# Three weight parts narrowed early and read back, the spread of 1/root on ScalarE, and the rows stored from ScalarE's queue

## The chip, the cores and the metric

One core of a Trainium2 chip runs the kernel; the other cores are idle. The metric is the time of one execution on the device in microseconds (us). Engines: PE (TensorE, matmuls), DVE (VectorE), ACT (ScalarE), POOL (GpSimd), SP (SyncE, which here only starts DMAs). Each engine carries out its own instructions in a fixed order, and they wait for one another on semaphores.

## The reference

Three stages, each the input of the next, in float32. The output of the third, 1792 rows of 768, is the result.

```python
# attention with a sigmoid: 4 batches, 12 heads, 448 positions, 64 wide
scores = scale * np.matmul(q, k.transpose(0, 1, 3, 2)) - np.log(S)
attn = 1.0 / (1.0 + np.exp(-scores))
x = np.matmul(attn, v)                       # then laid out as 1792 x 768
# gated dense layer (768 -> 1536 -> 768)
xn = x / np.sqrt(np.mean(x * x, axis=-1, keepdims=True) + 1e-06) * rms_g
g = xn @ w_gate
x = (g * (1.0 / (1.0 + np.exp(-g))) * (xn @ w_val)) @ w_out
# routed experts: 8 experts (768 -> 1024 -> 768), each row goes to its best one
logits = x @ w_gate2
e = np.argmax(logits, axis=1)                # gate_w = softmax(logits)[e]
out[row] = gate_w[row] * (np.maximum(x[row] @ w1[e], 0.0) @ w2[e])
```

## The kernel before

The work goes batch by batch. `moe1(b)` is the dense layer of batch b: 12 units that each make one slice of the gate (`pg`, by `w_gate`) and of the value (`pv`, by `w_val`), and then 6 output units (`oc` 0 to 5, bank `py`, by `w_out`). A unit has 4 pieces of 9 matmuls, a batch 72 pieces. Every product of float32 numbers is made of three matmuls over high and low parts (`three`, L299 to L301). The attention of batch b + 1 is spread over the pieces of batch b (`attention_due`), its matmuls between those of the dense layer. PE therefore has one order, written out by the Python code: whoever is late makes PE wait. `later(k, f)` puts f behind the k-th next piece.

PE's results lie in banks of PSUM. The dense layer has three banks `mm`, and in the output units one of them holds the logits of the routing (`logit_bank`), so that `py` goes back and forth between two, and so do the first units of the next batch until the logits are copied (L398).

The weights of the dense layer come as 64-bit words, 36 parts of 768 KB (`load_64`; two parts for each unit, 33 to 35 are the last of `w_out`). DVE narrows each part to float32 by three operations (L221, L225, L229), which the generator `conversions` gives out one at a time. 24 of the 108 stand in the attention of batch 0, then `operations_due(n)` after each piece n of batch 0. Parts 0 to 11 and 14 to 19 are held in the tiles h0 to h11, which later take the hidden values `hs`; the others pass through a ring of four. Each narrowed part is stored to DRAM (`w32d`), and batches 1 to 3 load it from there (`load_32`, L244). A part is then split: ACT casts the high part `wh` (L252), DVE subtracts the low part `wl` (L255).

What ends a gate's piece: ACT takes the sigmoid of the bank (L307), DVE multiplies (L308), and with that the bank is free. For a value: L313 on DVE, L314 on ACT, L315 on DVE. For an output unit: ACT copies the bank (`x2s`, L340), DVE makes its low part (L343) and a transposed copy `xr` (L346); SP stores `x2s` (L353), and after every second unit `rows` starts four DMAs that store `xr`, which has one buffer, as rows (L380). `logits` (L385) multiplies `x2s` one unit later.

The end of an attention: PE sums the squares `ss` of `x` into `pm` (L786), DVE begins 1/root (`va`, L791 to L799), and for b > 0 POOL refines it (L806 to L809, `ya`); DVE spreads it to `yb` (L814); PE turns `yb` into `prs` (L818), and `x` is scaled by it (L827 on DVE, L830 on ACT, L821 on DVE). In the routed experts L904 is ACT's activation of the first matmuls.

Every DMA that SP or ACT starts takes the next of eight semaphores in turn. Where the earlier DMA on that semaphore can still be under way, the engine that issues waits for its landing first.

Of the kernel before, what the change touches and what calls it, by code (L numbers as in the profile page):

```python
# [19 lines left out]
B, H, S, D = 4, 12, 448, 64  # L20
# [4 lines left out]
KF = FF // 128  # L25
# [3 lines left out]
CT = 112  # L29
NC = S // CT  # L30
# [9 lines left out]
NU = KF + KD  # L40
SP = mybir.EngineType.SP

HELD = 12

RAW = 3

RQK = 2
# [13 lines left out]

def operations_due(n):

    return 2 if n % 4 == 3 else 1


CONST = {}
# [31 lines left out]
def f32(ap):  # L99
    return ap.bitcast(F32)  # L100
# [3 lines left out]
def block_kernel(ctx, tc, qkp, qk, v, wg, wv, wo, g, gate, w1, w2, consts, out):  # L104
    nc = tc.nc
# [61 lines left out]
    def later(ticks, f, *a):  # L167

        due.setdefault(clock[0] + ticks, []).append((f, a))

    def tick():
        clock[0] += 1
        for f, a in due.pop(clock[0], []):
            f(*a)
# [22 lines left out]
    w64, w32, spl = {}, {}, {}  # L197

    def part_of(c):

        u, i = divmod(c, 2)
        if u < KF:
            return (wg, wv)[i][u]
        return wo[u - KF, :, KD * i : KD * i + KD]

    def load_64(c):
        r = rp.tile([128, DM, 2], I32, tag="w64", name="w64", bufs=RAW)
        words = part_of(c).rearrange("p c k -> p (c k)").bitcast(I32)
        nc.sync.dma_start(out=r, in_=words.rearrange("p (n t) -> p n t", t=2))
        w64[c] = r  # L210

    def narrow(c):

        r = w64.pop(c)
        lo, hi = r[:, :, 0], r[:, :, 1]
        if place[c] is not None:
            w = wp.tile([128, DM], F32, tag=f"h{place[c]}", name="w32h")
        else:
            w = wp.tile([128, DM], F32, tag="w32", name="w32", bufs=4)
        u = w.bitcast(I32)  # L220
        nc.vector.tensor_scalar(  # L221
            out=u, in0=hi, scalar1=3, scalar2=0x3FFFFFF8, op0=ALU.logical_shift_left, op1=ALU.bitwise_and
        )
        yield
        nc.vector.scalar_tensor_tensor(  # L225
            out=u, in0=lo, scalar=29, in1=u, op0=ALU.logical_shift_right, op1=ALU.bitwise_or
        )
        yield
        nc.vector.scalar_tensor_tensor(  # L229
            out=u, in0=hi, scalar=-0x40000000, in1=u, op0=ALU.bitwise_and, op1=ALU.bitwise_or  # L230
        )
        w32[c] = w
        if c < HELD:
            to_store.append((c, w))
        else:
            later(1, lambda: nc.sync.dma_start(out=w32d[c // 2][c % 2], in_=w))
        x = order.index(c) + RAW
        if x < 2 * NU:
            later(2 if c < 8 else 3, load_64, order[x])
        yield  # L240

    def load_32(n, i):
        w = wp.tile([128, DM], F32, tag="w32", name="w32", bufs=4)
        nc.sync.dma_start(out=w, in_=w32d[n % NU][i])  # L244
        w32[2 * n + i] = w

    def split_w(n, i):
        w = w32.pop(2 * n + i)
        h = wp.tile([128, KD, 128], F32R, tag="wh", name="wh", bufs=3)
        l = wp.tile([128, KD, 128], F32R, tag="wl", name="wl", bufs=3)  # L250
        w3 = w.rearrange("p (c k) -> p c k", k=128)
        nc.scalar.copy(out=h, in_=w3)  # L252

        def low():
            nc.vector.tensor_tensor(out=l, in0=w3, in1=f32(h), op=ALU.subtract)  # L255
            split_done[0] += 1
            if NU <= n + 1 < NU * B:
                load_32(n + 1, i)

        later(1, low)  # L260
        spl[n, i] = (h, l)

    place = {c: c if c < HELD else c - 8 if 14 <= c < 20 else None for c in range(2 * NU)}
    round_of = [c for c in range(2 * NU) if place[c] is None]
    order = list(range(14)) + [20, 21] + list(range(14, 20)) + list(range(22, 2 * NU))
    split_done = [0]
    to_store = []

    def conversions():
        for c in order:
            if place[c] is not None:
                before = c - 8 if c >= HELD else -1
            else:
                x = round_of.index(c)
                before = round_of[x - 4] if x >= 4 else -1
            while split_done[0] <= before:
                yield False
            for _ in narrow(c):  # L280
                yield True

    conv = conversions()

    def ahead(n, piece):
# [19 lines left out]
    def moe1(b):  # L305
# [32 lines left out]
        def out_copy(p, oc):  # L338
            h, l = (keep.tile([128, S], F32R, tag=f"x2_{k + oc % 2}", name="x2s") for k in (2, 4))
            nc.scalar.copy(out=h, in_=p)  # L340

            def rest():
                nc.vector.tensor_tensor(out=l, in0=p, in1=f32(h), op=ALU.subtract)  # L343
                if oc % 2 == 0:
                    pair[0] = keep.tile([128, S // 32, 2, 32], F32, tag="xr", name="xr")
                nc.vector.transpose(out=pair[0][:, :, oc % 2, :], in_=p.rearrange("p (j a) -> p j a", a=32))  # L346

            later(1, rest)
            x2_t[b, oc] = None, h, l

            def store():
                for k, x in enumerate((h, l)):
                    nc.sync.dma_start(out=x2s[b][k * KD + oc], in_=f32(x))  # L353
                if oc % 2:
                    rows(b, oc - 1, pair[0])

            later(2, store)
# [17 lines left out]
    def rows(b, oc, xr):  # L375

        to = x2d[0][b * S : (b + 1) * S, :DM].rearrange("(j a) (i r) -> i a j r", a=32, i=4)
        to = to[:, :, :, 32 * oc : 32 * oc + 64]
        for i in range(4):
            nc.sync.dma_start(out=to[i], in_=xr[32 * i : 32 * i + 32].rearrange("a j o r -> a j (o r)"))  # L380

    def logits(b, oc):

# [164 lines left out]
    def attention(b):  # L548
# [202 lines left out]
        for t in range(n_steps + 4 if b > 1 else 0):  # L751
            if t < n_steps:
                h, c = divmod(t, NC)
# [31 lines left out]
        for c in range(NC):  # L785
# [3 lines left out]
        ya = aq.tile([CT, NC], F32, tag="ya", name="ya")  # L789
# [4 lines left out]
            out=ta.bitcast(I32), in0=va.bitcast(I32), scalar1=1, scalar2=None, op0=ALU.logical_shift_right  # L794
        )
        nc.vector.tensor_scalar(
            out=ya.bitcast(I32), in0=ta.bitcast(I32), scalar1=-1.0, scalar2=float(0x5F3759DF), op0=ALU.mult, op1=ALU.add
# [13 lines left out]
            yield  # L811
            yield
        yb = aq.tile([CT, NC, 128], F32, tag="yb", name="yb")
        nc.vector.tensor_copy(out=yb, in_=ya.unsqueeze(2).to_broadcast([CT, NC, 128]))  # L814
        yield
        pr = sc_bank([128, S], "prs")
        for c in range(NC):
# [5 lines left out]
        before = None  # L823
        for c in range(KD):
# [3 lines left out]
                out=xt[c], in0=xt[c], scalar=g_sb[:, c : c + 1], in1=pr, op0=ALU.mult, op1=ALU.mult  # L828
# [4 lines left out]
            before = c, xh, xl  # L833
# [361 lines left out]


    att = {b: attention(b) for b in range(B)}
    for n in range(QS + 2):
        next(att[0])
        if n < RAW:  # L1200
            load_64(n)
# [4 lines left out]
        if n == 15:  # L1206
            nc.scalar.copy(out=gate_2[:, :, :E], in_=gate_sb)
            nc.vector.tensor_tensor(
                out=gate_2[:, :, E:], in0=gate_sb, in1=f32(gate_2[:, :, :E]), op=ALU.subtract
# [7 lines left out]
    for _ in att[0]:  # L1217
        tick()
        next(att[1])
        ahead_of += 1  # L1220
    gated.append(True)
    for b in range(B):
# [3 lines left out]
        for n, _ in enumerate(moe1(b)):  # L1226
            want = attention_due(b, n)
            while done < want:
                next(steps, None)
                done += 1  # L1230
            tick()
            if b == 0:
                if to_store:
                    c, w = to_store.pop(0)
                    nc.sync.dma_start(out=w32d[c // 2][c % 2], in_=w)
                for _ in range(operations_due(n)):
                    next(conv, None)
            elif n >= 2 and n % 2 == 0:
                next(routing, None)
            if b == 3:  # L1240
                if n == 0:
                    s_a.close()
                    s_r.close()
                    open_raw()
                    load_x(0)
                    e0 = own_expert(0)
                if n >= 2 and n % 2 == 0 and n < 2 * KD + 2:
                    load_row(w1, ph2["w1r"], e0, n // 2 - 1)
                if n == 49:
                    s_x.close()  # L1250
                    ph2["s1"], ph2["ring1"] = opened("ring1", side="right", reuse_waits="tile")
                if n in (62, 66):
                    split_block((n - 62) // 4)
# [167 lines left out]
```

## Time and profile before

| | |
|---|---|
| median of 3 runs | 979.60 us (979.58 to 979.75) |
| profiled execution | 979.25 us, span 977.4 us |
| PE busy | 957.3 us, 98% of the span |
| DVE busy | 635.9 us, 65% |
| ACT busy | 463.6 us, 47% |
| mean granted clock of PE | 0.996 |

The span goes from the first to the last instruction of the profiled execution; the remaining 1.85 us of its time lie around it. The profile shows each engine's instructions with their start and duration, and in brackets the idle time ahead of one with what ended it. PE is busy nearly always, so a gain or loss is found in its few waits. The granted clock is TensorE's, as a share of 2.4 GHz; 0.50 is 1.2 GHz.

### The profile page before, as it was taken

How to read it: one execution, taken by the hardware profiler on the slowest of the kernel's cores; microseconds unless marked ns; L12 is line 12 of the kernel's file. 1: busy time of each engine (PE TensorE's matmuls, PEld its weight loads, DVE VectorE, ACT ScalarE, POOL GpSimd, SP SyncE). 2: the span in 40 equal slices, each digit the busy share in tenths (PEclk: the TensorE clock that was granted, in tenths of full speed). 3: DMA queues.
4: the chain of work that ended last, by engine and by line, in shares of the span. 5: the costliest groups of instructions: out<-in, count | busy, mean ns of one | idle time of the engine just before them, and what ended most of it. 6: DMA issues, size and time to landing. Idle time of an engine off the chain costs nothing.

```text
span 977.4 us, 14479 instructions
## 1 busy us (share of the span) xinstructions
PE 957.3 (98%) x5334; PEld 831.5 (85%) x5334; DVE 635.9 (65%) x1103; ACT 463.6 (47%) x776; POOL 14.4 (1%) x43
## 2 busy tenths in 40 slices
PE   8989999989999999999999999999999999999996
PEld 4577777878999999899999999999889988889996
DVE  5688787786798875679886465654446734444454
ACT  6844444336878863578786333333223132232230
POOL 0000000010000001000000100000000000000000
PEclk9999999999999999999999999999999999999999
DMA  9938666669344344833522578433576659838633
GB/s 342 376 138 296 224 232 219 200 216 273 118 151 143 119 136 135 241 134 116 172 95 79 173 235 279 131 112 123 150 227 237 198 169 362 296 123 280 175 62 55
DMA packets 121455, 184.32 MB, mean 189 GB/s; under 512 B 62537, under 2 KB 79689, under 8 KB 121376
## 3 DMA queue, kind: packets, MB, share of 16 engines
q1 hardware_dynamic: 119344, 182.55, 57.9%
q8 instruction: 44, 0.72, 0.3%
q0 software_dynamic: 144, 0.53, 0.2%
q10 hardware_dynamic: 1888, 0.23, 0.2%
q14 instruction: 35, 0.29, 0.1%
HBM read 145.26 MB, written 37.88 MB: 187 GB/s over the span
## 4 chain that ended last, share of the span: by engine, by line
PE 92%; DVE 4%; DMA 1%; issue 1%; ACT 1%; SPq 0%; DVEq 0%; ACTq 0%
PE mm L299 21%; PE mm L301 20%; PE mm L300 20%; PE sc L299 4%; PE sc L300 4%; PE sc L301 4%; PE pav L687 3%; PE psc L667 3%; PE psc L559 2%; PE pav L592 2%; PE psc L560 2%; PE pav L594 2%; PE mm L667 1%; PE sc L1068 1%; PE mm L385 1%
## 5 line engine op out<-in xcount | busy, mean ns | idle before, releaser
L299 PE MATMUL mm<-xh,wh 128*128 128x448 f32 x576 | 213.9, 371 | 1.1 <-ACT xh L830 1.0
L300 PE MATMUL mm<-xl,wh 128*128 128x448 f32 x576 | 211.2, 367 | 0.2 <-DVE xl L821 0.2
L301 PE MATMUL mm<-xh,wl 128*128 128x448 f32 x576 | 210.8, 366 | 0.0
L255 DVE TENSOR_TENSOR wl<-w,wh 128x768 fp32r<-128x768 f32 x126 | 119.4, 948 | 30.1 <-ACT wh L252 25.7
L252 ACT CAST wh<-w 128x768 fp32r<-128x768 f32 x126 | 105.6, 838 | 64.0 <-DMA w<-w32d 22.3
L299 PEld LDWEIGHTS mm<-xh,wh 128*128 128x128 f32 x576 | 108.2, 188 | 22.4 <-issue 6.7
L301 PEld LDWEIGHTS mm<-xh,wl 128*128 128x128 f32 x576 | 108.2, 188 | 9.5
L300 PEld LDWEIGHTS mm<-xl,wh 128*128 128x128 f32 x576 | 108.2, 188 | 9.3 <-DVE xl L821 0.5
L299 PE MATMUL mm<-hs,wh 128*128 128x448 f32 x288 | 106.8, 371 | 0.3 <-DVE xr L346 0.3
L301 PE MATMUL mm<-hs,wl 128*128 128x448 f32 x288 | 106.1, 368 | 0.1
L300 PE MATMUL mm<-hs,wh 128*128 128x448 f32 x288 | 105.9, 368 | 0.0
L299 PE MATMUL sc<-hh,w2h 128*128 128x448 f32 (+1 forms) x200 | 72.0, 360 | 0.5 <-DVE yt L923 0.5
L300 PE MATMUL sc<-hl,w2h 128*128 128x448 f32 (+1 forms) x200 | 71.3, 356 | 0.0
L301 PE MATMUL sc<-hh,w2l 128*128 128x448 f32 (+1 forms) x200 | 71.2, 356 | 0.0
L299 PE MATMUL mm<-xd,w1h 128*128 128x448 f32 x192 | 70.9, 369 | 0.0
L300 PE MATMUL mm<-xd,w1h 128*128 128x448 f32 x192 | 70.1, 365 | 0.0
L301 PE MATMUL mm<-xd,w1l 128*128 128x448 f32 x192 | 70.1, 365 | 0.0
L569 ACT ACTIVATE a<-psc,logs 128x448 f32<-128x448 f32 x96 | 61.4, 640 | 16.6 <-PE psc L560 12.3
L904 ACT ACTIVATE hh<-mm 128x448 fp32r<-128x448 f32 x32 | 17.4, 544 | 105.0 <-PE mm L301 105.0
L299 PEld LDWEIGHTS mm<-hs,wh 128*128 128x128 f32 x288 | 54.6, 189 | 7.7 <-issue 1.2
L571 ACT ACTIVATE ah<-psc,logs 128x448 fp32r<-128x448 f32 x96 | 60.9, 635 | 0.0
L301 PEld LDWEIGHTS mm<-hs,wl 128*128 128x128 f32 x288 | 54.6, 190 | 5.1 <-DVE wl L255 0.5
(208 smaller groups left out, 1543.0 us busy)
## 6 DMA issues: line engine op xcount, KB each, us to landing
w<-w32d SPq DMA_DIRECT2D x108, 384.0 KB, 4.1
w1r<-in_w SPq DMA_DIRECT2D x24, 512.0 KB, 6.8
w2r<-in_w SPq DMA_DIRECT2D x32, 384.0 KB, 6.8
rqk<-in_qk SPq DMA_DIRECT2D x24, 480.0 KB, 3.5
x2s<-x2s SPq DMA_DIRECT2D x48, 224.0 KB, 2.4
xd<-x2s SPq DMA_DIRECT2D x8, 1344.0 KB, 11.8
w<-in_wg SPq DMA_DIRECT2D x12, 768.0 KB, 5.8
w<-in_wv SPq DMA_DIRECT2D x12, 768.0 KB, 5.6
```

The lines of the kernel that those rows point to most:

```text
L252: nc.scalar.copy(out=h, in_=w3)
L255: nc.vector.tensor_tensor(out=l, in0=w3, in1=f32(h), op=ALU.subtract)
L299: nc.tensor.matmul(p, wh, xh, start=(n == 0), stop=False)
L300: nc.tensor.matmul(p, wh, xl, start=False, stop=False)
L301: nc.tensor.matmul(p, wl, xh, start=False, stop=last)
L559: nc.tensor.matmul(psc, kh[:, keys], q2, start=True, stop=False)
L560: nc.tensor.matmul(psc, kl[:, keys], q2, start=False, stop=True)
L569: nc.scalar.activation(out=a, in_=psc, bias=logs, **act)
L571: nc.scalar.activation(out=ah, in_=psc, bias=logs, **act)
L592: nc.tensor.matmul(pav[h], v2[:, c, :], ah, start=(c == 0), stop=(c == 3))
L667: nc.tensor.matmul(to[o], r[head, k : k + D], r[head, :S], start=True, stop=True)
L687: nc.tensor.matmul(sums[p][k][halves[x]], v4[halves[i], c, x, :], a[halves[i]], start=(c == first), stop=(c == end))
```

## The change

Four things change. First, parts 33 to 35 are narrowed early, into the tiles h3 to h5 as soon as those are free of parts 3 to 5. They are stored, and batch 0 loads them back by `load_32` like the later batches. The order of the parts is now 0 to 12, 33, 13, 34, 20, 35, 21, 14 to 19, 22 to 32. Second, the narrowing is given out earlier: six operations more in the tail of attention 0 (two parts), then six a unit for five in the gate and value units. Third, for the attentions 1 to 3 ACT copies `yb` and not DVE, with one `yield` more, so that `prs` stands one piece later on PE. Fourth, the rows' DMAs are started by ACT and not by SP.

```diff
@@ -42,6 +42,8 @@
 
 HELD = 12
 
+AWAY = {33: 3, 34: 4, 35: 5}
+
 RAW = 3
 
 RQK = 2
@@ -61,7 +63,7 @@
 
 def operations_due(n):
 
-    return 2 if n % 4 == 3 else 1
+    return 1 + n % 2 if n < 4 * KF else 1
 
 
 CONST = {}
@@ -229,7 +231,8 @@
         nc.vector.scalar_tensor_tensor(
             out=u, in0=hi, scalar=-0x40000000, in1=u, op0=ALU.bitwise_and, op1=ALU.bitwise_or
         )
-        w32[c] = w
+        if c not in AWAY:
+            w32[c] = w
         if c < HELD:
             to_store.append((c, w))
         else:
@@ -254,7 +257,7 @@
         def low():
             nc.vector.tensor_tensor(out=l, in0=w3, in1=f32(h), op=ALU.subtract)
             split_done[0] += 1
-            if NU <= n + 1 < NU * B:
+            if NU <= n + 1 < NU * B or 2 * (n + 1) + i in AWAY:
                 load_32(n + 1, i)
 
         later(1, low)
@@ -262,16 +265,16 @@
 
 
 
-    place = {c: c if c < HELD else c - 8 if 14 <= c < 20 else None for c in range(2 * NU)}
+    place = {c: c if c < HELD else c - 8 if 14 <= c < 20 else AWAY.get(c) for c in range(2 * NU)}
     round_of = [c for c in range(2 * NU) if place[c] is None]
-    order = list(range(14)) + [20, 21] + list(range(14, 20)) + list(range(22, 2 * NU))
+    order = list(range(13)) + [33, 13, 34, 20, 35, 21] + list(range(14, 20)) + list(range(22, 33))
     split_done = [0]
     to_store = []
 
     def conversions():
         for c in order:
             if place[c] is not None:
-                before = c - 8 if c >= HELD else -1
+                before = place[c] if c >= HELD else -1
             else:
                 x = round_of.index(c)
                 before = round_of[x - 4] if x >= 4 else -1
@@ -377,7 +380,7 @@
         to = x2d[0][b * S : (b + 1) * S, :DM].rearrange("(j a) (i r) -> i a j r", a=32, i=4)
         to = to[:, :, :, 32 * oc : 32 * oc + 64]
         for i in range(4):
-            nc.sync.dma_start(out=to[i], in_=xr[32 * i : 32 * i + 32].rearrange("a j o r -> a j (o r)"))
+            nc.scalar.dma_start(out=to[i], in_=xr[32 * i : 32 * i + 32].rearrange("a j o r -> a j (o r)"))
 
     def logits(b, oc):
 
@@ -811,7 +814,11 @@
             yield
             yield
         yb = aq.tile([CT, NC, 128], F32, tag="yb", name="yb")
-        nc.vector.tensor_copy(out=yb, in_=ya.unsqueeze(2).to_broadcast([CT, NC, 128]))
+        if b == 0:
+            nc.vector.tensor_copy(out=yb, in_=ya.unsqueeze(2).to_broadcast([CT, NC, 128]))
+        else:
+            nc.scalar.copy(out=yb, in_=ya.unsqueeze(2).to_broadcast([CT, NC, 128]))
+            yield
         yield
         pr = sc_bank([128, S], "prs")
         for c in range(NC):
@@ -1217,6 +1224,7 @@
     for _ in att[0]:
         tick()
         next(att[1])
+        next(conv)
         ahead_of += 1
     gated.append(True)
     for b in range(B):
```

Three places in the order of the instructions carry the prediction. In the changed file the lines stand 2 to 7 further down: L223, L227 and L231 are the narrowing (L221, L225, L229), L258 is `wl` (L255), L311 the gate's multiplication (L308), L310 its sigmoid (L307), L343, L346 and L349 the copies of an output bank (L340, L343, L346), L383 the rows (L380), L828 and L834 are L821 and L827.

The first place is DVE at the begin of units 0 and 1 of batch 0, behind the end of attention 0: the narrowing of two parts (`w32h`) and the first gate's multiplication, before:

```order
L221 TENSOR_SCALAR w32h<-w_410 128x768
L255 TENSOR_TENSOR wl<-w32h,wh 128x768
L225 SCALAR_TENSOR_TENSOR w32h<-w_410,w32h 128x768
L229 SCALAR_TENSOR_TENSOR w32h<-w_410,w32h 128x768
L255 TENSOR_TENSOR wl<-w32h,wh 128x768
L221 TENSOR_SCALAR w32h<-w_449 128x768
L225 SCALAR_TENSOR_TENSOR w32h<-w_449,w32h 128x768
L308 TENSOR_TENSOR sg<-mm_123,sg 128x448
L229 SCALAR_TENSOR_TENSOR w32h<-w_449,w32h 128x768
```

and now:

```order
L223 TENSOR_SCALAR w32h<-w_486 128x768
L258 TENSOR_TENSOR wl<-w32h,wh 128x768
L227 SCALAR_TENSOR_TENSOR w32h<-w_486,w32h 128x768
L231 SCALAR_TENSOR_TENSOR w32h<-w_486,w32h 128x768
L223 TENSOR_SCALAR w32h<-w_657 128x768
L258 TENSOR_TENSOR wl<-w32h,wh 128x768
L227 SCALAR_TENSOR_TENSOR w32h<-w_657,w32h 128x768
L231 SCALAR_TENSOR_TENSOR w32h<-w_657,w32h 128x768
L311 TENSOR_TENSOR sg<-mm_123,sg 128x448
```

Parts 410 and 449 are now done in the tail of attention 0, and the gate's multiplication stands behind one operation more, the second L231.

The second place is DVE in the output units of batch 0, where the attention of batch 1 ends (`yb` to `xl`), before:

```order
L255 TENSOR_TENSOR wl<-w_1841,wh 128x768
L225 SCALAR_TENSOR_TENSOR w_1916<-w_1837,w_1916 128x768
L229 SCALAR_TENSOR_TENSOR w_1916<-w_1837,w_1916 128x768
L814 COPY yb<-ya 112x512
L221 TENSOR_SCALAR w_1952<-w_1907 128x768
L343 TENSOR_TENSOR x2s<-mm_124,x2s 128x448
L346 STREAM_TRANSPOSE xr<-mm_124 128x14x32
L255 TENSOR_TENSOR wl<-w_1916,wh 128x768
L225 SCALAR_TENSOR_TENSOR w_1952<-w_1907,w_1952 128x768
L827 SCALAR_TENSOR_TENSOR xt<-xt,g_sb,prs 128x448 x2
```

and now:

```order
L802 TENSOR_SCALAR va<-va 112x4
L258 TENSOR_TENSOR wl<-w_1819,wh 128x768
L346 TENSOR_TENSOR x2s<-mm_124,x2s 128x448
L349 STREAM_TRANSPOSE xr<-mm_124 128x14x32
L258 TENSOR_TENSOR wl<-w_1868,wh 128x768
L834 SCALAR_TENSOR_TENSOR xt<-xt,g_sb,prs 128x448 x2
```

The narrowing is gone from here, and so is `yb`. From the first L346 of the batch to the end of it 18 narrowing operations stood on DVE before, and 5 behind that place (L349) now.

The third place is ACT at the begin of batch 1: the attention of batch 2 (`a`, `ah`), the sigmoid of the batch's first gate (`sg`) and a weight's cast. Before:

```order
L569 ACTIVATE a<-psc,logs 128x448
L571 ACTIVATE ah<-psc,logs 128x448
L569 ACTIVATE a<-psc,logs 128x448
L571 ACTIVATE ah<-psc,logs 128x448
L307 ACTIVATE sg<-mm_124 128x448
L252 CAST wh<-w_2163 128x768
```

and now, with the semaphores that each waits for (DMAHW are those of the DMAs):

```order
L572 ACTIVATE a<-psc,logs 128x448 [waits PE_49]
L574 ACTIVATE ah<-psc,logs 128x448
L383 DMA x2d<-xr 32x14x64 [waits DMAHW6_49,DVE_49]
L383 DMA x2d<-xr 32x14x64 [waits DMAHW0_49]
L383 DMA x2d<-xr 32x14x64 [waits DMAHW1_49]
L383 DMA x2d<-xr 32x14x64 [waits DMAHW2_49]
L310 ACTIVATE sg<-mm_124 128x448
L255 CAST wh<-w_2169 128x768 [waits Activation_49]
```

The four DMAs of the rows now stand on ACT right ahead of the sigmoid, as they also do at the begin of batches 2 and 3. In batch 3 the fourth waits for the semaphore of the first (DMAHW3), and so for its landing.

## Rows read from the trace of the kernel before

**Rows 1.** The page, busy time of each engine.

```profile
PE 957.3 (98%) x5334; PEld 831.5 (85%) x5334; DVE 635.9 (65%) x1103; ACT 463.6 (47%) x776; POOL 14.4 (1%) x43
```

**Rows 2.** Timeline of PE, 190 to 220: start, us, [idle before <-releaser].

```profile
192.47 0.92 PE L786 MATMUL pm<-ones,ss 128*112 128x1 f32 x8 [0.62 <-DVE ss L612]
...
202.75 1.11 PE L818 MATMUL prs<-cst,yb 112*128 112x112 f32 x8 [1.55 <-DVE yb L814]
...
215.97 0.38 PE L385 MATMUL mm<-x2s,gate 128*16 128x448 f32 x1 [0.67 <-ACT x2s L340]
...
217.42 0.37 PE L385 MATMUL mm<-x2s,gate 128*16 128x448 f32 x1 [1.07 <-DVE x2s L343]
...
218.07 0.44 PE L299 MATMUL mm<-hs,wh 128*128 128x448 f32 x1 [0.28 <-DVE xr L346]
```

**Rows 3.** Windows: busy of PE, PEld, DVE, ACT, POOL, clock, DMA share, GB/s.

```profile
218.00:220.00 2.00, 1.83 (x5) 1.40 (x6) 1.97 (x3) 0.00 (x0) 0.00 (x0) 0.72 0.93 269
220.00:222.00 2.00, 2.00 (x7) 1.74 (x7) 1.18 (x2) 0.67 (x1) 0.00 (x0) 0.50 1.15 326
222.00:224.00 2.00, 2.00 (x11) 1.82 (x10) 1.49 (x2) 1.33 (x3) 0.00 (x0) 0.93 1.24 213
...
70.00:75.00 5.00, 5.00 (x26) 4.54 (x25) 5.00 (x8) 1.05 (x2) 0.00 (x0) 1.00 1.06 414
```

**Rows 4.** Timeline of DVE around 202.

```profile
202.17 0.43 DVE L814 COPY yb<-ya 112x512 f32<-112x512 f32 x1 [2.38 <-POOL ya L809]
```

**Rows 5.** DVE's groups by line: busy us, mean ns, idle before.

```profile
L229 DVE SCALAR_TENSOR_TENSOR w32h<-w,w32h 128x768 int32<-128x768 int32 x18 | 17.2, 954 | 0.4
...
L221 DVE TENSOR_SCALAR w32h<-w 128x768 int32<-128x768 int32 x18 | 10.0, 555 | 10.3 <-DMA w<-in_wg 10.0 <-DMA w<-in_wv 0.3
```

**Rows 6.** Timelines of DVE and PE, unit 1 of batch 0.

```profile
65.89 0.62 DVE L308 TENSOR_TENSOR sg<-mm,sg 128x448 f32<-128x448 f32 x1
...
66.56 0.47 PE L299 MATMUL mm<-xh,wh 128*128 128x448 f32 x1
```

**Rows 7.** Timelines of DVE, PE and ACT at the begin of batches 1 and 2.

```profile
236.62 0.62 DVE L308 TENSOR_TENSOR sg<-mm,sg 128x448 f32<-128x448 f32 x1
...
237.29 0.47 PE L299 MATMUL mm<-xh,wh 128*128 128x448 f32 x1
...
408.42 0.55 ACT L307 ACTIVATE sg<-mm 128x448 f32<-128x448 f32 x1
...
411.46 0.62 DVE L308 TENSOR_TENSOR sg<-mm,sg 128x448 f32<-128x448 f32 x1
...
412.13 0.47 PE L299 MATMUL mm<-xh,wh 128*128 128x448 f32 x1
```

**Rows 8.** Timeline of SP: two of the rows' stores.

```profile
393.78 2.00 SPq L380 DMA_DIRECT2D x2d<-xr  x4
...
579.64 7.40 SPq L380 DMA_DIRECT2D x2d<-xr  x4
```

**Rows 9.** L956 (ACT's issues), then landings: L380 whole, 578:590; L353 404:410.

```profile
L956 ACTq DMA_DIRECT2D out<-yp x6: 323/386/458, 965.6 to 971.5; - x6
...
DMA to landing us min/median/max: 2.3/4.3/11.9
...
DMA to landing us min/median/max: 6.9/10.6/11.9
...
DMA to landing us min/median/max: 4.4/4.7/5.1
```

**Rows 10.** Timelines of DVE and PE, first unit of batch 3.

```profile
581.86 0.62 DVE L308 TENSOR_TENSOR sg<-mm,sg 128x448 f32<-128x448 f32 x1 [1.84 <-ACT sg L307]
...
585.16 0.37 PE L299 MATMUL mm<-xh,wh 128*128 128x448 f32 x1
```

**Rows 11.** The page, DMA issues: KB each, median us to landing.

```profile
w2r<-in_w SPq DMA_DIRECT2D x32, 384.0 KB, 6.8
```

**Rows 12.** Timeline of ACT, begin of the routed experts.

```profile
717.47 0.54 ACT L904 ACTIVATE hh<-mm 128x448 fp32r<-128x448 f32 x1 [3.52 <-PE mm L301]
```

## The prediction

> **What bounds the kernel now.** The page comes first: TensorE (PE) is busy 98% of the span [rows 1], and its instructions stand in one fixed order, so only its waits, its clock and a lateness that the change would bring can move the time. Next came the waits of PE by releaser, and then the timeline of PE where they lie. Outside the start of attention 0 and the tail of the routed experts there is one cluster of any size: the output units of the first batch, between 192 and 219 us [rows 2]. There PE waits 0.62 us for `ss`, 1.55 for `yb`, and 0.67, 1.07 and 0.28 for `x2s` and `xr`. In windows of 2 us, the granted clock right behind that cluster is 0.72, 0.50 and 0.93 [rows 3]: 0.50 is 1.2 of 2.4 GHz, and what PE did before it fell was to stand still three times within 3 us. Last came the timelines of VectorE (DVE) and ScalarE (ACT) at the seams between units and batches, since there the change puts new work.
>
> **What it takes away.** In the first output units DVE also narrows weights. After the first L346 of the batch 18 narrowing operations still stood on DVE before; now 5 do, 13 fewer (counted in the order). A part costs one L221 (0.555 us) and two operations like L229 (0.954) [rows 5], a mean of 0.82, so 10.7 us of DVE's work leaves this stretch. `yb` leaves it too: there DVE stood 2.38 us behind L814, waiting for POOL's last `ya` [rows 4], with the narrowing, the copies `x2s` and `xr` and L827 queued behind. What this gives PE, wait by wait [rows 2]:
> - `ss` 0.62: DVE was late by more narrowing than that. Gone.
> - `prs` 1.55: it stands one piece later, nine matmuls or about 1.86 us, and ScalarE's copy can start when `ya` is done. Gone, with a margin of some 0.3.
> - `x2s`, `x2s` and `xr`: 0.67 + 1.07 + 0.28 = 2.02. Gone: in the second piece of the order the next `x2s` and `xr` (L346, L349 in the changed file) stand behind `va` and one weight's L258, and not behind L225, L229, `yb` and L221.
> - the clock: 2 us at 0.72, 2 at 0.50 and 2 at 0.93 lose 0.56 + 1.00 + 0.14 = 1.70 [rows 3]. Gone if the three waits ahead of it are.
>
> Together 5.89 us, at least 4.2 (without the clock).
>
> **What it adds.**
>
> *Start.* The narrowing moves to the tail of attention 0 (two parts, where DVE stood idle for PE) and to units 0 to 11, with six operations a unit for five. In the first piece of the order the L308 (in the changed file L311) that frees the first gate bank stands behind one more operation, the second L229. Before, L308 ran 65.89 to 66.51 and PE's matmul into that bank began at 66.56 [rows 6]: no slack. So one operation passes whole, 0.95. The bounds are 0.3 (part of the tail's head start reaches this far) and 3 (rival 3).
>
> *Seams 0 to 1 and 1 to 2.* The four DMAs of the third rows now stand on ACT right ahead of the L307 (in the changed file L310) of the new batch's first unit (third piece of the order). Behind them wait that sigmoid, the weight cast L252, two activations of the attention and the cast of `v`; behind those DVE's L545 and L308; behind L308 the next bank of PE. That chain has no slack at either seam [rows 7]: L308 ends at 237.24 and PE goes on at 237.29; L308 ends at 412.08 and PE at 412.13. So what the issues cost ACT passes to PE. No row of before shows ACT issuing rows. The nearest are its six stores of `out`, 323 to 458 ns, median 386 [rows 9], and SyncE's four rows, 2.00 us [rows 8]. Four by 386 are 1.54, of which I let 0.2 lie beside the tail of the activation ahead: 1.35 at the first seam. At the second the third and fourth issue also need the semaphores of the last `x2s` stores, which landed 4.4 to 5.1 us after issue [rows 9], just about when ACT, at 408.42 [rows 7], gets there: 1.7. The bounds at each are 0.5 (the issues overlap the running activations) and 2.5.
>
> *Seam 2 to 3.* Here no attention runs beside, and the same L308 ends at 582.48, before PE wants the bank at 585.16 [rows 10]: 2.68 of slack. But the fourth issue waits on a semaphore that the first one raises only when it lands. First issue, landing, last issue, sigmoid, L308: by these durations PE stands still for about the landing less 4.2 us. Rows landed in 2.3 to 11.9 us over the run, median 4.3, and in 6.9 to 11.9 at this seam, where the reloads of the routed experts fill the queues [rows 9]. I take a landing halfway between 4.3 and 6.9, 5.6, because ACT's queue does not stand behind SyncE's: 1.4. The bounds are 0 and 7.7.
>
> That SyncE's four issues took 2.00 us in one place and 7.40 in the other [rows 8] shows how the seam's traffic slows such a store. The Trainium skill, in "DMA: Bandwidth & Descriptors", section "Issuing engines are not separate DMA queues", says that DMAs begun by ScalarE, SyncE or GpSimd run on the same 16 engines and interleave, and that starting them elsewhere saves only the time of issue. By that rule the rows land no sooner from ACT; with the seam's own least landing of 6.9 the term is 2.7 and not 1.4, and the sum 981.6. No run so far shows a row stored by ACT, so it cannot be decided here.
>
> *Into the routed experts.* After batch 3 the last row's issue waits for a load of `w2r`, which lands in 6.8 us [rows 11], and behind it stands L904, ahead of which ACT had 3.52 us of idle [rows 12]. Between 0 and 6.8 − 3.5 = 3.3 I take 0.6, because that load is issued well ahead.
>
> *Small ones.* `xr` has one buffer and its rows now leave up to 1.5 us (four issues) later; an output pair takes about 15 us (8 pieces of 1.86), landing 4.3 [rows 9], so the next transpose rarely waits: 0.2, from 0 to 1.5. A fall of the clock behind one of the new stalls, a quarter of the 1.70 above: 0.4. The copy of `yb` on ACT (DVE took 0.43 [rows 4]) finds ACT busy for 47% of the span [rows 1] and costs nothing; if ACT is full there, prs has 0.3 of margin. The three reloads of 384 KB in batch 0 go where parts are loaded anyway; if they are late, ACT's cast is, and then PE.
>
> **The sum.** Losses: 0.95 + 1.35 + 1.7 + 1.4 + 0.6 + 0.2 + 0.4 = 6.60. Gains: 5.89. The profiled execution (979.25 us) would go to 979.96. Its time is 0.35 below the median of the runs (979.60), so the median goes to about 980.3. With 0.2% (1.96 us) as the least that a measurement of this kernel tells from no change, this is no change: two effects of about six microseconds that cancel.
>
> **The rivals.**
> - *1, faster.* ACT's issues run beside its activations and the rows land in the run's median of 4.3. Then the seams cost 0.5, 0.5 and 0, the routed experts nothing, no clock falls: 5.89 − 0.95 − 1.0 − 0.2 = 3.74 less, 975.9. For it: the issue's 323 to 458 ns [rows 9] are time of a sequencer, and ACT's arithmetic may go on meanwhile. Against: the sigmoid comes behind them in the same queue.
> - *2, slower.* At seam 2 to 3 the first row lands as late as the slowest did there, 11.9: the stall is 7.7, the clock falls for the price seen before (1.70), and the sum is 0.71 − 1.4 + 7.7 + 1.7 = 8.7 more, 988.3. For it: every row landed there in 6.9 or more [rows 9]. Against: those stood in SyncE's queue behind the reloads. With no clock lost, the median is over 0.2% slower from a landing of about 6.9 on (a stall of 2.7).
> - *3, slower by the start.* DVE is busy 5.00 of 5 us from 70 to 75 and the DMA engines 1.06 [rows 3]; six operations a unit add 0.82 us to each, and units 0 to 3 have no attention of the next batch to fill PE. If units 1 to 3 each pass that on, 2.5 more: 982.8. Against: two parts are done in the tail of attention 0, so three of PE's banks start with that lead. It decides once DVE's lateness at a gate is more than about 1.5 us.
>
> **How the numbers follow.** Forecast 0.36 (its own range 978.5 to 982.5), rival 1 0.30, rival 2 0.24, rival 3 0.10. Faster by over 0.2% are rival 1 (0.28 of it) and the low edge of the forecast (0.05): 0.33. Within 0.2%: 0.28 of the forecast, 0.02 of rival 1 and 0.02 of rival 3: 0.32. Slower: the rest, 0.35. The range of 8 in 10 goes from 975.3 (a little below rival 1) to 986.0 (a stall of 5.4 at seam 2 to 3 with the clock kept up, or less with it lost), which leaves out about a tenth at either end.
>
> **What the changed profile would show.** Right: no waits of PE by `ss`, `yb`, `x2s` or `xr` between 190 and 220, and the clock at 1.00 there. PE waits of about 1.0 near 66, and of 1.3 to 1.7 at the first unit of batches 1 and 2, released by L311, with four issues on ACT's queue ahead of its sigmoid. One longer wait at the first unit of batch 3, the length of a row's landing less 4.2. Wrong: the waits at 200 to 219 stay or move into the next output unit (DVE was not the cause), or PE waits at the seams are nothing (the issues are free), or PE waits in units 1 to 4, behind DVE or a weight that has not come.

## The result, and the profile after

The changed kernel takes 988.52 us (median of six, 986.34 to 994.22), the kernel before 979.59 (median of six): a ratio of 1.0102, with a 95% interval of 1.0086 to 1.0117. It is slower by 1.0%; the forecast was no change, 980.3, and a range that ended at 986.0. The profiled execution is the slowest of the six, 994.22 with a span of 992.4, 15.0 us above the span before, so its terms add up to more than the median's 8.9.

PE's timeline after, with each wait that is not also in the kernel before or is changed (start, us, instruction, [idle before <-releaser]):

```profile
68.51 0.47 PE L302 MATMUL mm<-xh,wh 128*128 128x448 f32 x1 [0.95 <-DVE sg L311]
...
102.73 1.76 PE L690 MATMUL pav<-a,rv 64*64 64x448 f32 x6 [2.44 <-DVE xt L715]
...
240.61 0.47 PE L302 MATMUL mm<-xh,wh 128*128 128x448 f32 x1 [1.30 <-DVE sg L311]
...
417.07 0.47 PE L302 MATMUL mm<-xh,wh 128*128 128x448 f32 x1 [1.25 <-DVE sg L311]
...
578.85 0.47 PE L302 MATMUL mm<-hs,wh 128*128 128x448 f32 x1 [0.36 <-ACT wh L255]
579.84 0.47 PE L304 MATMUL mm<-hs,wl 128*128 128x448 f32 x1 [0.32 <-DVE wl L258]
...
594.97 0.74 PE L302 MATMUL mm<-xh,wh 128*128 128x448 f32 x1 [3.49 <-DVE sg L311]
...
735.27 0.95 PE L407 MATMUL mi<-cst,lt 16*112 16x8 f32 x8 [1.87 <-ACT lt L401]
```

The five waits of [rows 2] have no counterpart: between 103 and 240 PE waits for nothing. In the windows of the same execution (columns as in [rows 3]) the clock is 1.00 where it fell before, and falls in three new places:

```profile
102.00:104.00 2.00, 1.27 (x6) 0.30 (x6) 2.00 (x5) 0.00 (x0) 0.00 (x0) 0.50 0.85 278
104.00:106.00 2.00, 2.00 (x7) 1.45 (x5) 1.97 (x4) 0.00 (x0) 0.00 (x0) 0.50 0.87 349
106.00:108.00 2.00, 2.00 (x7) 1.74 (x7) 1.73 (x4) 1.50 (x3) 0.00 (x0) 0.50 0.62 203
108.00:110.00 2.00, 2.00 (x10) 1.79 (x8) 1.97 (x3) 0.28 (x1) 0.00 (x0) 0.80 1.02 347
...
220.00:224.00 4.00, 4.00 (x22) 3.49 (x21) 2.04 (x4) 1.40 (x3) 0.00 (x0) 1.00 0.94 245
...
594.00:596.00 2.00, 1.03 (x3) 0.95 (x4) 1.61 (x3) 0.98 (x2) 0.00 (x0) 0.50 1.07 379
596.00:598.00 2.00, 2.00 (x7) 1.78 (x6) 1.13 (x2) 1.46 (x3) 0.00 (x0) 0.50 0.89 166
598.00:600.00 2.00, 2.00 (x7) 1.74 (x7) 0.96 (x1) 0.26 (x1) 0.00 (x0) 0.50 0.91 257
600.00:602.00 2.00, 2.00 (x11) 1.86 (x10) 0.07 (x1) 0.65 (x2) 0.00 (x0) 0.92 0.98 303
...
736.00:738.00 2.00, 2.00 (x10) 1.80 (x10) 1.82 (x6) 0.37 (x1) 0.00 (x0) 0.71 1.07 387
738.00:740.00 2.00, 2.00 (x7) 1.78 (x6) 0.83 (x5) 0.23 (x1) 0.00 (x0) 0.50 1.10 350
740.00:742.00 2.00, 2.00 (x12) 1.84 (x11) 0.00 (x0) 0.34 (x1) 0.00 (x0) 0.94 1.15 345
```

Each fall goes with a wait of PE: in windows of 0.5 us the clock falls within the wait of 2.44 us (near 102.0) and that of 3.49 (near 593.5), and 1.4 us behind the end of the one of 1.87. The fall that every run shows in the tail of the routed experts is left out. What a fall loses is the time at the lower clock by its share, without the part in which PE stood still anyway (0.73 us behind 102, 0.97 behind 594): about 3.0, 2.7 and 1.7 us.

ACT's timeline shows the four issues at the seams, of batch 1 to 2, of 2 to 3, and into the routed experts. The column behind the start is the time of the whole group on ACT's queue:

```profile
411.06 0.99 ACTq L383 DMA_DIRECT2D x2d<-xr  x2
411.53 0.62 ACT L574 ACTIVATE ah<-psc,logs 128x448 fp32r<-128x448 f32 x1
412.09 1.27 ACTq L383 DMA_DIRECT2D x2d<-xr  x2
413.41 0.54 ACT L310 ACTIVATE sg<-mm 128x448 f32<-128x448 f32 x1 [1.25 <-issue]
...
585.16 8.51 ACTq L383 DMA_DIRECT2D x2d<-xr  x4
593.71 0.54 ACT L310 ACTIVATE sg<-mm 128x448 f32<-128x448 f32 x1 [9.07 <-DMA x2d<-xr]
...
727.15 6.28 ACTq L383 DMA_DIRECT2D x2d<-xr  x4
733.54 0.54 ACT L911 ACTIVATE hh<-mm 128x448 fp32r<-128x448 f32 x1 [7.63 <-PE mm L304]
```

At 411 the first two issues run beside the attention's activations, and ACT then stands 1.25 us. At 585 ACT does nothing for 9.07 us: the sigmoid's releaser is the landing of a row. At 727 the profile names PE as the releaser of L911, but ACT's own issues fill the gap until 733.43. DVE's timeline ahead of PE's 2.44 us at 102.73 (part 35 begins at 93.13), and SyncE's issue of the load of part 35 with its landing:

```profile
86.20 0.56 DVE L223 TENSOR_SCALAR w<-w 128x768 int32<-128x768 int32 x1 [0.77 <-DMA w<-in_wg]
...
93.13 0.56 DVE L223 TENSOR_SCALAR w32h<-w 128x768 int32<-128x768 int32 x1 [3.10 <-DMA w32d<-w]
...
102.06 0.62 DVE L715 TENSOR_TENSOR xt<-pav,xt 128x448 f32<-128x448 f32 x1
...
82.97 1.44 SPq L211 DMA_DIRECT2D w<-in_wo  x1
...
DMA to landing us min/median/max: 10.1/10.1/10.1
```

Between 93.13 and that `xt` DVE is idle for only 0.17 us, and PE waits for it. The profile names a store (`w32d<-w`) as what ended the 3.10 us, but the landings say otherwise: the load of part 35, asked for at 82.97, landed 10.1 us later, at about 93.05. The store of a former part that this operation also waits for was issued at 77.33 and landed 6.4 us later, long before.

### The profile page after: what moved, and what is told of

Its sections match the earlier page's. It is cut to its first block, busy times and chain, and to the rows that moved or that the text cites. A ratio compares the mean times of both kernels' runs of the same rounds, so it can differ in the third digit from the quotient of the medians.

```text
span 992.4 us, 14469 instructions
## 1 busy us (share of the span) xinstructions
PE 964.6 (97%) x5334; PEld 834.3 (84%) x5334; DVE 637.0 (64%) x1100; ACT 464.5 (47%) x779; POOL 14.1 (1%) x43
## 4 chain that ended last, share of the span: by engine, by line
PE 84%; DVE 7%; DMA 4%; ACT 2%; issue 1%; ACTq 1%; SPq 0%; DVEq 0%
PE mm L302 19%; PE mm L304 18%; PE mm L303 18%; PE sc L302 4%; PE sc L303 4%; PE sc L304 4%; PE pav L690 3%; PE psc L670 2%; PE pav L595 2%; PE psc L562 2%; PE psc L563 2%; PE pav L597 1%; DMA x2d<-xr 1%; DVE wl L258 1%; DVE xt L834 1%
## 5 line engine op out<-in xcount | busy, mean ns | idle before, releaser
L258 DVE TENSOR_TENSOR wl<-w,wh 128x768 fp32r<-128x768 f32 x126 | 119.2, 948 | 30.6 <-ACT wh L255 23.8
L255 ACT CAST wh<-w 128x768 fp32r<-128x768 f32 x126 | 105.2, 837 | 32.2 <-PE mm L303 13.7
L911 ACT ACTIVATE hh<-mm 128x448 fp32r<-128x448 f32 x32 | 17.4, 543 | 108.8 <-PE mm L304 106.4
L317 ACT CAST hs<-sg 128x448 fp32r<-128x448 f32 x48 | 27.3, 568 | 79.4 <-DVE sg L316 76.7
```

The lines of the kernel that those rows point to most:

```text
L317: nc.scalar.copy(out=hs[:, 0, :], in_=t)
```

## The experiments

Two theories stood against each other: A, that the rows on ACT's queue are the loss, and B, that the early narrowing is. Ratios are to the kernel before, with 95% intervals, each timed beside it on the same chip.

**Rows back on SyncE** (run rows_sp), the changed kernel with

```diff
-            nc.scalar.dma_start(out=to[i], in_=xr[...
+            nc.sync.dma_start(out=to[i], in_=xr[...
```

> The changed kernel with the rows' DMAs back on SyncE; all else as changed. Theory A (the rows on ScalarE's queue are the loss): the four waits of PE at the seams, 1.30, 1.25, 3.49 and 1.87 us, go, and with them the clock falls behind the last two (about 2.7 and 1.7), together 12.3; the median goes from 988.5 to about 976. Theory B (the early narrowing is the loss, with the DVE wait for a store at 93 us): only the 2.5 us of the first two seams come back, about 986.

Measured: 977.50 us, ratio 0.9968 (0.9957 to 0.9979). The waits at 240, 417, 595 and 735 are gone, and so are the two clock falls behind the last two. Theory A holds: with the rows back on SyncE the change is a gain of 0.3%. The wait at 68 and the one behind 93 are still there (0.97 and 2.42, the latter with a clock fall), and the times spread from 975.08 to 979.88.

**Rows on ScalarE alone** (run rows_act), the kernel before with

```diff
-            nc.sync.dma_start(out=to[i], in_=xr[...
+            nc.scalar.dma_start(out=to[i], in_=xr[...
```

> The kernel before with one edit: the rows' DMAs on ScalarE. Theory A: the same four waits and two clock falls appear, about 12 us, 991 to 992. Theory B: the two seams with no slack alone, 2.5 us, about 982.

Measured: 998.02 us, ratio 1.0188 (1.0175 to 1.0201), 17.6 us more. Theory A holds, and its price was too low. PE's timeline of this run shows the four waits, and two more in the first batch:

```profile
214.25 0.47 PE L301 MATMUL mm<-hs,wl 128*128 128x448 f32 x1 [1.36 <-DVE wl L255]
...
232.52 0.44 PE L299 MATMUL mm<-xh,wh 128*128 128x448 f32 x1 [1.35 <-DVE xr L346]
...
243.43 0.47 PE L299 MATMUL mm<-xh,wh 128*128 128x448 f32 x1 [0.98 <-DVE sg L308]
...
420.11 0.47 PE L299 MATMUL mm<-xh,wh 128*128 128x448 f32 x1 [1.85 <-DVE sg L308]
...
597.71 0.74 PE L299 MATMUL mm<-xh,wh 128*128 128x448 f32 x1 [4.12 <-DVE sg L308]
...
737.77 0.95 PE L404 MATMUL mi<-cst,lt 16*112 16x8 f32 x8 [1.69 <-ACT lt L398]
```

The first two are a late low part of a weight (`wl`) and the single `xr` buffer, in the stretch that the narrowing still fills here; the expectation had neither in its 12. The clock falls behind the last two waits, and behind the cluster at 220 as in the kernel before.

**The spread of 1/root alone** (run yb_only), the kernel before with

```diff
-        nc.vector.tensor_copy(out=yb, in_=ya.unsqueeze(2).to_broadcast([CT, NC, 128]))
+        if b == 0:
+            nc.vector.tensor_copy(out=yb, in_=ya.unsqueeze(2).to_broadcast([CT, NC, 128]))
+        else:
+            nc.scalar.copy(out=yb, in_=ya.unsqueeze(2).to_broadcast([CT, NC, 128]))
+            yield
```

> The kernel before with one edit: ScalarE spreads 1/root for the attentions 1 to 3, and prs stands one piece later. If the wait of VectorE for POOL was what made x2s and xr late, all of prs 1.55, x2s 0.67 and 1.07, xr 0.28 and the clock 1.70 go: about 974.5. If the narrowing operations were, only the 1.55 goes: about 978.

Measured: 979.61 us, ratio 0.9993 (0.9984 to 1.0002), no difference. PE's timeline of this run says why:

```profile
214.40 0.38 PE L385 MATMUL mm<-x2s,gate 128*16 128x448 f32 x1 [0.70 <-ACT x2s L340]
...
217.57 0.37 PE L385 MATMUL mm<-x2s,gate 128*16 128x448 f32 x1 [2.79 <-DVE x2s L343]
```

The 1.55 us at `prs` went, and the wait for `x2s` grew from 1.07 [rows 2] to 2.79: DVE was as late as before, and PE only reached the next place sooner. Neither expectation foresaw that.

**The early narrowing alone** (run narrow_only), the change with rows on SyncE and `yb` on DVE, so without the last two of its four parts.

> The change without its other two parts: the parts 33 to 35 early and read back and the narrowing earlier, rows on SyncE, 1/root spread by VectorE. If the narrowing operations made the output units late: prs's wait of up to 1.55 may stay (VectorE still waits for POOL), the rest of 4.3 goes, 0.95 is lost at 68 us: about 976.3, and 981 to 982 where the wait for a store at 93 us and its clock fall (5.4) come. If they were not: 979.6 plus 0.95 or more, 980.5 and over.

Measured: 977.79 us, ratio 0.9971 (0.9962 to 0.9981), between the two numbers of the first case and on its side. There is no wait at `prs` although DVE still copies `yb`; POOL's chain to `ya`, at whose end that copy stands, took 4.0 us here and 5.6 in the kernel before, where DVE was narrowing beside it. That this is why is likely, but not shown. The profiled execution (981.22, the slowest of its runs, which begin at 975.25) has 1.16 at 69 us and 2.43 at 103.

**The stores of parts 3 to 5 first** (run store_first), rows_sp with

```diff
-                c, w = to_store.pop(0)
+                c, w = to_store.pop(next((k for k, s in enumerate(to_store) if s[0] in AWAY.values()), 0))
```

> Rows on SyncE, and the stores of the parts 3 to 5, whose tiles the early parts 33 to 35 take, go out first. In the profiles so far VectorE stands 2.8 to 3.3 us at 93 us ahead of the first operation of part 35, in one for the store of part 5, in one for the load of part 35. Theory S (the store is late): that wait, PE's 2.4 behind it and the clock fall of 1.7 to 3 go, from 977.5 to about 973. Theory L (the load is late because the DMA engines are full from 65 to 95): VectorE's wait stays at about 2.8, the time at about 977.

Measured: 977.51 us, ratio 0.9985 (0.9975 to 0.9995), no gain over rows_sp (977.50, 0.9968). DVE waits at the same operation, now by name for the load of part 35:

```profile
91.88 0.56 DVE L223 TENSOR_SCALAR w32h<-w 128x768 int32<-128x768 int32 x1 [2.38 <-DMA w<-in_wo]
```

Theory S falls. It rested on the name in the profile; in the changed kernel, too, the wait ends with the landing of this load.

**Six operations a unit only from unit 4 on** (run rate_late), rows_sp with

```diff
-    return 1 + n % 2 if n < 4 * KF else 1
+    return 1 + (n % 4 == 3 or n % 2 and 16 <= n < 4 * KF)
```

> Rows on SyncE, and the narrowing as before, five operations a unit, in units 0 to 3, six only from unit 4 on; 8 narrowing operations at most are left for the output units. Theory L: with fewer loads asked for between 65 and 95 the wait at 93 us goes, and also the 0.95 us at 68, since one operation less stands ahead of the first gate: 977.5 less 0.95, 2.4 and 1.7 is about 972.5. Theory S: only 0.95 goes, 976.5.

Measured: 973.51 us (972.79 to 974.02), ratio 0.9944 (0.9931 to 0.9956). The time is that of theory L. This is the fastest version here, 0.56% faster than the kernel before. What PE still waits for by releaser (us in all, times, longest):

```profile
PE prs L825 <- ACT a L681: 1.2, 1, 1.2
PE mm L302 <- ACT xh L837: 1.0, 1, 1.0
PE pm L789 <- DVE ss L615: 0.9, 1, 0.9
...
PE mm L302 <- DVE sg L311: 0.3, 1, 0.3
```

The wait at 103 is gone, that at 68 fell from 0.97 to 0.29, and the clock falls nowhere ahead of the tail. Only the wait for `ss` at 193 is back, 0.90 (0.62 in [rows 2]). The reason that theory L gave is not what the trace shows, though: between 65 and 95 six loads of parts are asked for here as in the changed kernel, and the DMA engines are nearly as full (share 0.86 to 1.01 in windows of 5 us from 70 to 95, against 0.99 to 1.02). What differs is the time between the asking for part 35 and DVE's coming to it:

```profile
81.65 0.46 SPq L211 DMA_DIRECT2D w<-in_wo  x1
...
DMA to landing us min/median/max: 8.6/8.6/8.6
...
94.50 0.55 DVE L223 TENSOR_SCALAR w32h<-w 128x768 int32<-128x768 int32 x1
```

Here DVE comes 12.85 us after the issue and does not wait. In the changed kernel it was ready at 90.03, 7.06 us after the issue, and even the landing there, about 93.05, would be early enough for 94.50. The run changes DVE's work and the loads together, so their shares are not told apart.

**The rows two pieces later on ScalarE** (run rows_late), the changed kernel with

```diff
-                    rows(b, oc - 1, pair[0])
+                    later(2, rows, b, oc - 1, pair[0])
```

> The changed kernel with the rows still on ScalarE, but two pieces later, so behind the sigmoid of the new batch's first gate. If the place ahead of that sigmoid is what costs: the waits at 240, 417 and 595 us (1.30, 1.25, 3.49 and the clock 2.7) go, from 988.5 to about 980 (the wait into the routed experts stays). If the issues on ScalarE cost wherever they stand: about 988 again, with the waits behind other instructions.

Measured: 984.18 us, ratio 1.0053 (1.0040 to 1.0066). The three waits of PE at the seams are gone, so it is the place ahead of the sigmoid that makes them. ACT still stands nearly as long, but behind its sigmoid, as its timeline at the seam 2 to 3 shows:

```profile
583.28 8.10 ACTq L383 DMA_DIRECT2D x2d<-xr  x3
591.42 0.57 ACT L317 CAST hs<-sg 128x448 fp32r<-128x448 f32 x1 [7.37 <-DMA x2d<-xr]
```

No wait of PE follows from the late cast `hs`. The time came to 984 and not 980. The wait into the routed experts (1.44, with a clock fall) and the losses of the start were in the 980 already; new are 1.96 us of waits for `xr` and `x2s` between 210 and 230 (the longest 1.11 at 229). Some 2 us more are not explained.

**One set of rows back on SyncE** (run rows_seam_sp), the changed kernel with

```diff
-            nc.scalar.dma_start(out=to[i], in_=xr[...
+            (nc.sync if b == 2 and oc == KD - 2 else nc.scalar).dma_start(out=to[i], in_=xr[...
```

> The changed kernel with one of the twelve sets of rows back on SyncE, the third of batch 2. If its fourth DMA's wait for the landing of the first is the 3.49 us at 595 and the clock fall behind it (2.7): 6.2 less, about 982.3. If the wait is that of the first unit's bank for other reasons (the reloads of the routed experts fill the queues): it stays, 988.

Measured: 982.97 us, ratio 1.0037 (1.0024 to 1.0050), where the changed kernel has 1.0102. Four DMAs of 48 cost about 6 us. The wait at 595 and its clock fall are gone, the other three stay (1.16, 1.74, 1.36).

**rate_late with `yb` on DVE again** (run late_no_yb).

> The run rate_late (973.5) with 1/root spread by VectorE again. If the move of that copy is needed for the 1.55 us of prs: 1.0 to 1.6 more, about 975. If VectorE, free of narrowing, does it in time (narrow_only showed no wait at prs): the same, 973.5.

Measured: 974.14 us, ratio 0.9944 (0.9931 to 0.9958): the same. With the narrowing away the copy of `yb` may stay on DVE. Its profile has no wait at `prs`, but one of 1.15 us at 594 for a step of the routing on DVE, which rate_late has not.

**rate_late without the early parts** (run late_no_away), with

```diff
-AWAY = {33: 3, 34: 4, 35: 5}
+AWAY = {}
-    order = list(range(13)) + [33, 13, 34, 20, 35, 21] + list(range(14, 20)) + list(range(22, 33))
+    order = list(range(14)) + [20, 21] + list(range(14, 20)) + list(range(22, 2 * NU))
```

> The run rate_late without the early narrowing and reading back of the parts 33 to 35 (order of the parts as before); the ring of four then keeps 13 narrowing operations behind the first transposed copy of the output units, not 4. If it is the narrowing in the output units that made x2s and xr late: waits of 1 to 4 us between 200 and 220 come back, with a clock fall, 976 to 978. If the copy of 1/root was: no waits, 973.5 (or a little less, without the reloads).

Measured: 977.45 us, ratio 0.9975 (0.9965 to 0.9984) against 0.9944, 3 us (by ratio) to 4 us (by medians) more than rate_late. PE's timeline has the waits of the output units again:

```profile
205.21 1.15 PE L825 MATMUL prs<-cst,yb 112*128 112x112 f32 x8 [0.58 <-ACT yb L820]
...
217.90 0.37 PE L388 MATMUL mm<-x2s,gate 128*16 128x448 f32 x1 [1.66 <-DVE x2s L346]
```

So it is the narrowing on DVE that made these late, with `yb` on ACT too, and the reading back of three parts is worth its DMAs. The clock did not fall behind these waits.

**rate_late with the rows on ScalarE** (run late_rows_act).

> The run rate_late (973.5) with the rows on ScalarE, the change's one part that theory A blames: the waits at the three seams and into the routed experts with two clock falls, 10 to 12 us, 983.5 to 985.5. If the loss needed the overloaded start beside it: under 5 us, below 978.5.

Measured: 986.41 us, ratio 1.0060 (1.0046 to 1.0074) against 0.9944, 11 to 13 us over rate_late. The rows cost as much in a kernel with no trouble at its start: 1.25, 1.13, 3.40 and 1.51 us of waits of PE and a clock fall behind the last. Waits and fall add up to about 11. The second clock fall of the expectation, behind the 3.40, did not come.

## Why the prediction was wrong, point by point

**What it takes away: right.** All five waits and the clock fall between 192 and 224 are gone, 5.89 us as forecast. Its cause was right for the narrowing (late_no_away) and wrong for `yb`: the copy alone is worth nothing (yb_only), and beside the narrowing it is not needed (late_no_yb). The prediction counted 1.55 us for it that moving the narrowing brings by itself.

**The start: half of it.** The 0.95 at the first gate bank came as 0.95. What failed is that the sum had no term for a load that DVE waits for; the only place for it was rival 3, with a chance of a tenth. PE's wait came at 102.7, behind the last piece of unit 4, which is still in the stretch that the prediction named as a sign of being wrong. But it was not rival 3's 0.82 us passed on by each gate: DVE, ahead by the added operations, came to part 35 at 90.03, the load landed at about 93.05, and DVE, 3.10 us later by that, was late for the next attention's `xt`. The DMA engines were full (share 0.94 to 1.02 in each window of 5 us from 70 to 100), but they were nearly so in the kernel before (0.79 to 1.06 from 70 to 95). With the clock that is 5.4 us of the profiled execution. The runs of rows_sp spread over 4.8 us and those of rate_late over 1.2, so this lateness probably differs from one execution to the next; that was not looked at further.

**The seams 0 to 1 and 1 to 2: right.** 1.30 and 1.25 against 1.35 and 1.7. An issue took longer than forecast (median 0.518 us in the row of L383, forecast 0.386), but at both seams two of the four ran beside activations, so the sizes agree partly by luck. The wait for the `x2s` stores that made the second dearer did not come: they had landed by 411.4, and the third issue went out at 412.09.

**The seam 2 to 3: mechanism right, size wrong, and this is the step that failed first.** The term of 1.4 rested on a landing of 5.6 us, "because ACT's queue does not stand behind SyncE's". That did not help it: the fourth issue, at 593.4, which waits for the landing of the first, came 8.2 us after the first at 585.16, and 8.2 lies in the 6.9 to 11.9 of SyncE's rows at this seam [rows 9]. The DMA engines were full meanwhile (share 1.06 from 585 to 594). 8.2 less 4.2 is 4.0, and PE waited 3.49. Over the run the landings, in the view of the rows' line, are these for the changed kernel and then for rows_sp:

```profile
DMA to landing us min/median/max: 2.3/4.9/12.3
```

```profile
DMA to landing us min/median/max: 2.2/4.0/11.7
```

Rows land no sooner from ACT. The Trainium skill says in "DMA: Bandwidth & Descriptors", section "Issuing engines are not separate DMA queues", that DMAs run on the same 16 engines whichever engine starts them, and here the trace agrees (median 4.9 against 4.0 us). The clock fall that goes with it (2.7) was priced at 0.4 for all places together. The run rows_seam_sp shows the price of this one set of rows directly, about 6 us.

**Into the routed experts: size wrong.** 0.6 was taken between 0 and 3.3; PE waited 1.87, and the clock fell for 1.7 more. The step that failed is "that load is issued well ahead": SyncE started it at 727.73, 0.6 us behind the first row, and it landed 5.4 us later, so that ACT's four issues took 6.28 us.

**The sum.** Seam and experts were forecast at 2.0 with a quarter of a clock fall (0.4), and came to 3.49 + 2.7 + 1.87 + 1.7 = 9.8; DVE's wait for the load of part 35 was not in the sum and came to 5.4. Those two explain nearly all of the 14 us between forecast and profiled execution; 0.68 are two late weights at 579, which rows_sp does not have, and about 1 us arose before 36 us, where only waits of the same size as before are seen (that start differs by as much between the other runs). This is the slowest execution. Over all runs, the rows' terms together (1.35, 1.7, 1.4, 0.6, 0.2 and 0.4) were forecast at 5.65 and cost 11 by medians (988.52 less 977.50 of rows_sp) or 13 by ratios (1.0102 less 0.9968); the other terms were forecast as a gain of 4.94 and gave 3.1 (0.32% in rows_sp). So the rows are most of what went wrong. Rival 2's number, 988.3, is near the median, but by luck: its stall was to be 7.7. The range's upper end was also worked out wrongly: a stall of 5.4 gives 986.0 with 1.70 of clock lost; with the clock kept up it takes 7.1.

## What to carry to other kernels

A DMA issue on a computing engine costs little (here 0.31 to 0.88 us each) only while no earlier DMA is waited for; where the issue must wait for a landing, everything behind it on that engine waits as well (here 8.51 us for four), so look which semaphore each issue takes and who holds it. Place such an issue behind the engine's last urgent instruction, or leave it on an engine with nothing to lose. When work is moved earlier to relieve an engine, check when that engine now comes to each load, and how long such a load takes to land there: giving out the same operations a few units later was worth another 2 to 4 us.

## What the runs showed that I had not expected

- A wait of PE of 3.49 us at the seam 2 to 3 went with about 6.7 us at 0.50 in the changed kernel, from within the wait on, and one of 3.40 at the same place in late_rows_act with none: the clock stayed at 1.00 through the wait and behind it. What PE did in the 15 us before was the same. Of the shorter ones, 1.44 us in rows_late was followed by a fall and 1.66 us in late_no_away by none. So the price of the stall at this seam differs by 2.7 us, and its length alone does not tell which it will be.
- Removing one wait can lengthen the next by nearly the same amount: 1.55 off at `prs`, 1.72 more at `x2s` (yb_only).
